# Attention scores as 64x64 products in the quarters of the array, with four scaled tables and a slot of its own for the diagonal

## Chip, cores and metric

The kernel runs on one core of one Trainium2 chip. The metric is the device time of one execution in microseconds (us); less is better. One profiled execution of the kernel before gives the trace that is read here.

## The reference

Three layers follow each other: banded attention, a mixture of experts with soft slots, and a mixture of experts with Sinkhorn weights. All arrays are float32. The parts that the change touches are the scores of the attention and, in the last layer, some small steps that prepare an expert.

```python
# attention: batch 4, 8 heads, 576 positions, head size 64, window 128
scores = q @ k.T / 8
bias = -slopes[h] * |i - j|, slopes[h] = 2.0 ** -(h + 1)
mask = (i - j >= 0) & (i - j < 128)
attn = softmax(where(mask, scores + bias, -1e9))
x = (attn @ v), heads laid side by side -> [2304, 512]

# layer 2: 8 experts with 4 slots each, F = 1024
logits = x @ phi                               # [2304, 32]
slot_input = softmax(logits over rows).T @ x
slot_out[e] = relu(slot_input[e] @ w1[e]) @ w2[e]
x = softmax(logits over slots) @ slot_out

# layer 3: 8 experts, F = 1024
P = exp(x @ w_gate); 8 rounds of: rows to sum 1, columns to sum 1, times N / E
out = sum over e of P[:, e] * (relu(x @ m1[e]) @ m2[e])
```

## The kernel before, in words

The order of all instructions is written out by hand; each engine works through its own queue in that order and waits by semaphores. Loads and stores are issued from SyncE's queue (SP).

**Attention.** The 576 rows of a batch are 9 chunks of 64. Two batches (j = 0, 1) are worked on together, so there are 18 steps t, and a step has two half-steps s = 2t + hf, each for four heads: two groups g = 2 hf + gg of two heads a = 0, 1. `load_nat(t)` (L124) loads a chunk of k and of q, both batches below each other on the 128 partitions, with two loads each; from the third step on, `scale_q` (L178) multiplies q on GpSimd by -(2^(2g-2)), and in the first two steps the copy out of PSUM does it. `emit_tr` (L147) turns them with TensorE transposes, a pair of heads at a time, into kT and qT. kT holds six chunk places; qT is block-diagonal: VectorE writes head a = 0 to partitions 0 to 63 and columns 0 to 63 (L172), ScalarE writes head a = 1 to partitions 64 to 127 and columns 64 to 127 (L173), and the other two blocks stay zero from one memset (L453). So one full 128x128 product (`emit_qk`, L202) gives the scores of both heads of a pair: four products for a half-step, against up to 192 columns of kT. float32 products are two passes each, so a half-step shows eight matmul records.

`emit_sm` (L206) adds one table of distances (rel_sb, 128x192, the same for all heads), scales, and takes the row minimum, by a VectorE instruction for each pair of group and batch (L221). `emit_exp` (L227), `emit_nm` (L234: divide by the sum, L240), `emit_pt` (L242: transposes L251, copies L252) and `emit_pv` (L255, L276) follow, each a half-step or more later, so that half-step s has the scores of s, the division of s - 1, the transposes of s - 2 and the product with v of s - 3. `emit_pv` uses products with 64 output columns, and with 64 or 128 rows. `emit_x` (L287) and `group` (L357) turn the finished chunks and gather the slots of layer 2. Weights of layer 2 are loaded ahead, one part in each half-step.

**Layer 2** ends with `prep_w1(0)`, which prepares expert 0 of layer 3.

**Layer 3** has 72 rounds m = 9 e + n of seven products each (`step`, L1078; each product is 12 matmuls at L1045). Generators run beside the rounds; at each of the seven places of a round one `next` is taken (L1194). They hold the gate and Sinkhorn (L895, L925) and the preparation of the next expert: `prep_w1` (L678) computes 32 matmuls (L682) into the PSUM tile m, takes the row maximum (L686), spreads it over a diagonal (`spread`, L550: tile dg = identity times the maximum, L553), sums the diagonal over partitions with a matmul of ones (`largest`, L557), takes a power of two (L86), scales the result into sh and sl (L701, L702), and copies these by 16 small transfers into stk (L710). `prep_w2a` (L572) then does the same with the maximum of m2 and its own dg. The tile dg has the tag "sl" in the pool mp, so dg and sl share one place.

```python
def spread(am):
    dg = mp.tile([128, 128], F32, tag="sl", name="dg", bufs=1)
    nc.vector.tensor_scalar_mul(dg, idn, am)
    return dg
...
    sl = mp.tile([128, 256], F16, tag="sl", name="sl", bufs=1)
```

Of the kernel before, what the change touches and what calls it, by code (L numbers as in the profile page):

```python
# [24 lines left out]
def tile_kernel(ctx: ExitStack, tc: tile.TileContext, q, k, v, phi, w1, w2, w_gate, m1, m2, rel, out):  # L25
# [69 lines left out]
    with tc.manual_schedule():  # L95
        with ExitStack() as ab:
# [5 lines left out]
            with ExitStack() as at:  # L102
# [13 lines left out]
                phi_sb = late.tile([128, DC, NS], F32, name="phi_sb")  # L116
                rel_sb = sp.tile([128, 192], F32, name="rel_sb", bufs=1)

                qT = one.tile([128, 4, 2, 128], F32, name="qT")

# [3 lines left out]
                def load_nat(t):  # L124
                    bp, c = divmod(t, NCH)
                    for nm, src in (("k", k), ("q", q)):
                        nt_ = nat.tile([128, H, D], F32, tag=nm + "n", name=nm + "n")
                        for j in range(2):
                            nc.sync.dma_start(
                                out=nt_[CH * j:CH * j + CH],  # L130
                                in_=src[2 * bp + j, :, CH * c:CH * c + CH, :].rearrange("h i d -> i h d"),
                            )
                        natt[nm, t] = nt_
                    if t > 1:
                        scale_q(t)

# [9 lines left out]

                def emit_tr(t, nm, gs=range(4), late_=False):  # L147
                    if nm == "q" and t < 2 and len(gs) > 1:
                        for g in gs:
                            emit_tr(t, nm, [g], g % 2 == 1)  # L150
                        return
                    src = natt[nm, t]
                    ps = ps_t.tile([128, 4, 128], F32, tag="pt", name="pt")
                    for i, g in enumerate(gs):
                        nc.tensor.transpose(
                            ps[:, i, :], src[:, 2 * g:2 * g + 2, :].rearrange("p a d -> p (a d)"), idn)
                    pv_ = ps[:, 0:len(gs), :].rearrange("p g (j i) -> p g j i", j=2)
                    if nm == "k":
                        sl_ = t % 4
                        nc.vector.tensor_copy(out=kT[:, :, :, CH * sl_:CH * sl_ + CH], in_=pv_)  # L160
                        if sl_ < 2 and t >= 4:
                            nc.scalar.copy(out=kT[:, :, :, CH * (sl_ + 4):CH * (sl_ + 5)], in_=pv_)
                    else:
                        g0, g1 = gs[0], gs[-1] + 1
                        if t < 2:
                            if not late_:
                                nc.vector.tensor_scalar_mul(qT[0:64, g0, :, 0:64], pv_[0:64, 0], scales[g0])
                            nc.scalar.mul(qT[64:128, g0, :, 64:128], pv_[64:128, 0], scales[g0])
                            if late_:
                                nc.vector.tensor_scalar_mul(qT[0:64, g0, :, 0:64], pv_[0:64, 0], scales[g0])  # L170
                            return
                        nc.vector.tensor_copy(out=qT[0:64, g0:g1, :, 0:64], in_=pv_[0:64])  # L172
                        nc.scalar.copy(out=qT[64:128, g0:g1, :, 64:128], in_=pv_[64:128])  # L173


                scales = [-(2.0 ** (2 * g - 2)) for g in range(4)]

                def scale_q(t):  # L178
                    for g in range(4):
                        x_ = natt["q", t][:, 2 * g:2 * g + 2, :]  # L180
                        nc.gpsimd.tensor_scalar_mul(x_, x_, scales[g])  # L181

# [7 lines left out]
                def emit_qk(s):  # L190
                    t, hf = divmod(s, 2)
                    c = t % NCH
                    nch = min(c, 2) + 1
                    k0 = CH * ((t - nch + 1) % 4)
                    k1 = k0 + CH * nch
                    col = 192 - (k1 - k0)
                    ps = []
                    for gg in range(2):
                        g = 2 * hf + gg
                        ps.append(ps_s.tile([128, 2, 256], F32, tag="s", name="s"))  # L200
                        for j in range(2):
                            nc.tensor.matmul(ps[gg][:, j, col:192], lhsT=qT[:, g, j, :], rhs=kT[:, g, j, k0:k1],  # L202
                                             start=True, stop=True)
                    sc[s] = (ps, col)

                def emit_sm(s):  # L206
# [8 lines left out]
                    for hh in range(4):  # L215
                        gg, j = divmod(hh, 2)
                        w = 192 - col
# [3 lines left out]
                        nc.vector.tensor_tensor_reduce(  # L221
                            out=runs[hh], in0=ps[gg][:, j, col:192],
                            in1=rel_sb[:, col:192], scale=2.0 ** -(4 * hf + 2 * gg + 1), scalar=3e38,
                            op0=ALU.add, op1=ALU.min, accum_out=mx[:, hh:hh + 1])
# [226 lines left out]
                load_nat(0)  # L451
                nc.sync.dma_start(out=rel_sb, in_=rel)
                nc.gpsimd.memset(qT, 0.0)  # L453
                load_nat(1)
# [5 lines left out]
                emit_tr(0, "k")  # L460
                warm(None, ps, idn, 3)
                emit_tr(0, "q", range(0, 2))
                emit_tr(0, "q", range(2, 4))

# [82 lines left out]
            wsum = {}  # L547
            bound = {}

            def spread(am):  # L550

                dg = mp.tile([128, 128], F32, tag="sl", name="dg", bufs=1)
                nc.vector.tensor_scalar_mul(dg, idn, am)  # L553
# [124 lines left out]
            def prep_w1(e, pool=None, tag=None):  # L678
                ps = pool.tile([128, 512], F32, tag=tag, name="m") if pool is not None else pmt
                for dc in range(DC):  # L680
                    for kk in range(4):
                        nc.tensor.matmul(ps[32 * kk:32 * kk + 32, 0:256], lhsT=st[:, dc, :],  # L682
                                         rhs=w1_at("m1", e, dc, 256 * kk, 256),
                                         start=(dc == 0), stop=(dc == DC - 1), tile_position=(0, 32 * kk))
                am = mp.tile([128, 1], F32, tag="am1", name="am1")
                nc.vector.tensor_reduce(out=am, in_=ps[:, 0:256], axis=AX.X, op=ALU.max, apply_absolute_value=True)  # L686
                dg = spread(am)
# [197 lines left out]
            with ExitStack() as ms:  # L885
                ap_ = ms.enter_context(tc.tile_pool(name="acc", bufs=1, reuse_waits="tile"))
                acc = ap_.tile([128, NT, DM], F32, name="acc")

                pmt = pm.tile([128, 512], F32, name="m")
                sp = ms.enter_context(tc.tile_pool(name="sums", bufs=1, reuse_waits="tile"))  # L890
                pz = ms.enter_context(tc.tile_pool(name="pz", bufs=2, reuse_waits="tile", space=PSUM))
# [3 lines left out]
                def gate():  # L895
# [14 lines left out]
                    for g in range(NG):  # L910
                        nc.tensor.matmul(ps[:, 32 * g:32 * g + 32], lhsT=cTf[:, g, :],
                                         rhs=sgb.rearrange("p a b -> p (a b)"), start=True, stop=True)
                    l2 = ps[:, 0:NT * E]
                    mx = mp.tile([128, 1], F32, tag="mx", name="mx")
# [325 lines left out]
```

## Time and profile before

| what | us |
|---|---|
| median of 3 runs | 984.17 |
| lowest, highest | 983.91, 984.69 |
| profiled execution, its own time | 984.86 |
| profiled execution, span from first to last instruction | 983.1 |
| TensorE busy | 950.5 (97%) |
| VectorE busy | 744.9 (76%) |
| ScalarE busy | 624.4 (64%) |
| GpSimd busy | 574.3 (58%) |

The span is counted from the first instruction; all times of rows are from there. Attention's half-steps run from about 8 us to 158 us, layer 2 to 212 us, layer 3 from there to the end. In rows PE is TensorE's matmul, PEld its weight load, DVE VectorE, ACT ScalarE, POOL GpSimd and SP SyncE; SPq is SyncE's queue, which issues the loads. "x8" counts records that follow each other. A matmul's record is as long as its passage through the array, so records overlap: when the next one can start is read from the starts.

### The profile page before, as it was taken

How to read it: one execution, taken by the hardware profiler on the slowest of the kernel's cores; microseconds unless marked ns; L12 is line 12 of the kernel's file. 1: busy time of each engine (PE TensorE's matmuls, PEld its weight loads, DVE VectorE, ACT ScalarE, POOL GpSimd, SP SyncE). 2: the span in 40 equal slices, each digit the busy share in tenths (PEclk: the TensorE clock that was granted, in tenths of full speed). 3: DMA queues.
4: the chain of work that ended last, by engine and by line, in shares of the span. 5: the costliest groups of instructions: out<-in, count | busy, mean ns of one | idle time of the engine just before them, and what ended most of it. 6: DMA issues, size and time to landing. Idle time of an engine off the chain costs nothing.

```text
span 983.1 us, 24146 instructions
## 1 busy us (share of the span) xinstructions
PE 950.5 (97%) x9341; PEld 814.4 (83%) x9341; DVE 744.9 (76%) x1924; ACT 624.4 (64%) x1529; POOL 574.3 (58%) x685
## 2 busy tenths in 40 slices
PE   8999999889799999999999999999999999999997
PEld 7887886447588888888888888888888888888886
DVE  6988896675697687777777777877777777777775
ACT  5877884746467678766666665766476656664542
POOL 2222210204488568947884797499658956995442
PEclk9999999999899999999999999999999999999999
DMA  8999997970200220031005001300220020001222
GB/s 174 257 226 219 254 281 284 368 267 2 96 1 2 94 90 1 2 109 76 1 2 182 2 1 54 131 2 2 89 95 2 1 94 5 2 2 28 60 44 65
DMA packets 94497, 90.07 MB, mean 92 GB/s; under 512 B 63664, under 2 KB 67632, under 8 KB 94384
## 3 DMA queue, kind: packets, MB, share of 16 engines
q1 hardware_dynamic: 94384, 88.54, 30.9%
q8 instruction: 73, 1.20, 0.5%
q14 instruction: 40, 0.33, 0.1%
HBM read 81.97 MB, written 4.72 MB: 88 GB/s over the span
## 4 chain that ended last, share of the span: by engine, by line
PE 67%; DVE 2%; ACT 0%; issue 0%
PE x L1045 34%; PE y L1045 26%; PE z L973 6%; PE m L682 1%; DVE acc L1059 1%; DVE ops L986 0%; DVE sl L702 0%; ACT sh L701 0%; PE m L557 0%; DVE ar L696 0%; DVE w1i L92 0%; DVE w1p L91 0%; DVE w1p L90 0%; DVE acc L1057 0%; PE m L936 0%
## 5 line engine op out<-in xcount | busy, mean ns | idle before, releaser
L1045 PEld LDWEIGHTS <-ops 128*128 128x128 f16 x6048 | 593.4, 98 | 77.2 <-issue 5.5
L1005 POOL TENSOR_TENSOR ops<-s,ops 128x512 f16<-128x512 f32 x287 | 331.9, 1159 | 234.4 <-ACT ops L1002 196.6
L1045 PE MATMUL x<-w2h,ops 128*128 128x256 f16 x2304 | 415.5, 273 | 4.0 <-DVE acc L1059 3.1
L1045 PE MATMUL y<-w2h,ops 128*128 128x256 f16 x1728 | 319.5, 273 | 0.3 <-POOL ops L1005 0.2
L1002 ACT CAST ops<-s 128x512 f16<-128x512 f32 x288 | 177.8, 618 | 218.5 <-DVE s L998 216.0
L1045 PE MATMUL x<-w2l,ops 128*128 128x256 f16 x1152 | 314.8, 274 | 0.0
L1045 PE MATMUL y<-w2l,ops 128*128 128x256 f16 x864 | 235.6, 273 | 0.0
L1059 DVE SCALAR_TENSOR_TENSOR acc<-x,pe,acc 128x256 f32<-128x256 f32 x252 | 121.8, 483 | 71.1 <-PE x L1045 70.0
L983 ACT ACTIVATE ops<-z 128x512 f16<-128x512 f32 x216 | 128.6, 596 | 36.9 <-PE z L973 34.0
L986 DVE SCALAR_TENSOR_TENSOR ops<-z,ops 128x512 f16<-128x512 f32 x216 | 147.0, 681 | 0.0
L1059 DVE SCALAR_TENSOR_TENSOR acc<-y,pe,acc 128x256 f32<-128x256 f32 x189 | 91.4, 484 | 61.4 <-PE y L1045 60.5
L640 POOL TENSOR_TENSOR w2l<-w,w2h 128x256 f16<-128x256 f32 x168 | 112.9, 676 | 0.0
L998 DVE SCALAR_TENSOR_TENSOR s<-z,r 128x512 f32<-128x512 f32 x144 | 98.2, 682 | 10.3 <-ACT r L994 7.1
L998 DVE SCALAR_TENSOR_TENSOR s<-z,s 128x512 f32<-128x512 f32 x144 | 98.1, 681 | 1.4 <-POOL t L640 0.7
L181 POOL TENSOR_SCALAR qn<-qn 128x128 f32<-128x128 f32 x64 | 33.8, 536 | 100.5 <-DMA qn<-in_q_dram 70.7
L973 PE MATMUL z<-ct,stk 128*128 128x256 f16 x576 | 86.8, 274 | 3.2 <-DVE ops L986 2.5
L643 ACT CAST w2h<-w 128x256 f16<-128x256 f32 x168 | 67.0, 402 | 2.3 <-POOL w L640 2.3
L973 PEld LDWEIGHTS <-stk 128*128 128x128 f16 x576 | 55.6, 98 | 13.1 <-DVE ops L986 3.3
L230 ACT ACTIVATE et<-et,mx 128x192 f32<-128x192 f32 (+2 forms) x144 | 61.3, 434 | 1.2 <-DVE mx L221 1.1
L202 PE MATMUL s<-kT,qT 128*128 128x192 f32 (+2 forms) x288 | 50.2, 317 | 0.1
L221 DVE CUSTOM_DVE_ANT_0 et<-s,rel_sb 128x192 f32<-128x192 f32 (+2 forms) x144 | 40.1, 326 | 8.5 <-PE s L202 8.0
L202 PEld LDWEIGHTS s<-kT,qT 128*128 128x128 f32 x288 | 43.7, 191 | 3.4 <-issue 3.4
(196 smaller groups left out, 949.6 us busy)
## 6 DMA issues: line engine op xcount, KB each, us to landing
w<-in_moe_w_dram SPq DMA_DIRECT2D x68, 512.0 KB, 6.4
w<-in_moe_w_dram SPq DMA_DIRECT2D x14, 2048.0 KB, 8.3
kn<-in_k_dram SPq DMA_DIRECT2D x36, 128.0 KB, 5.4
qn<-in_q_dram SPq DMA_DIRECT2D x36, 128.0 KB, 4.9
v<-in_v_dram SPq DMA_DIRECT2D x18, 256.0 KB, 5.1
out_dram<-acc SPq DMA_DIRECT2D x34, 128.0 KB, 2.4
w<-in_moe_w_dram SPq DMA_DIRECT2D x2, 1024.0 KB, 8.4
stk<-sh SPq DMA_DIRECT2D x56, 16.0 KB, 1.8
```

The lines of the kernel that those rows point to most:

```text
L202: nc.tensor.matmul(ps[gg][:, j, col:192], lhsT=qT[:, g, j, :], rhs=kT[:, g, j, k0:k1], start=True, stop=True)
L230: nc.scalar.activation(out=runs[hh], in_=runs[hh], func=AF.Exp, bias=mx[:, hh:hh + 1], scale=-1.0, accum_out=sm[:, hh:hh + 1])
L640: nc.gpsimd.tensor_tensor(out=out_, in0=x_, in1=y_, op=ALU.subtract)
L643: nc.scalar.copy(out=hi[:, i, r], in_=src[:, r])
L973: nc.tensor.matmul(ps[:, i], lhsT=stk[e][:, 128 * ft:128 * ft + 128], rhs=ct.rearrange("p (a n) t -> p a n t", a=2)[:, :, n, :], start=Tru ...
L983: nc.scalar.activation(out=ops_[m][:, k_, 0], in_=zb(m, i, j), func=AF.Relu)
L986: nc.vector.scalar_tensor_tensor(out=ops_[m][:, k_, 1], in0=zb(m, i, j), scalar=0.0, in1=ops_[m][:, k_, 0], op0=ALU.max, op1=ALU.subtract)
L998: nc.vector.scalar_tensor_tensor(out=new_sum(m, nm), in0=zb(m, i, j), scalar=0.0, in1=o, op0=ALU.max, op1=op)
L1002: nc.scalar.copy(out=ops_[m][:, k_, 0], in_=sm_[m, nm])
L1005: eng.tensor_tensor(out=ops_[m][:, k_, 1], in0=sm_[m, nm], in1=ops_[m][:, k_, 0], op=ALU.subtract)
L1045: nc.tensor.matmul(out_, lhsT=a_[:, k_, l_, i, :], rhs=r_[:, k_, i, :], start=(first and j == 0), stop=(j == 11), skip_group_check=True)
L1059: nc.vector.scalar_tensor_tensor(out=o, in0=ps, scalar=pe_[e][:, t:t + 1], in1=o, op0=ALU.mult, op1=ALU.add)
```

## The change

Each head's scores become two products of 64x64 of their own. qT holds 64 columns in place of 128 and no zeros, and is written by one VectorE copy of 128 partitions; ScalarE's copy, GpSimd's scaling and memset and the scaling copies of the first two steps go. The heads of the second batch are loaded swapped within each pair, by two loads with a stride in place of one, so that its head a lies in the other 64 rows of the array. The eight products of a half-step name their quarter by (first row, first column): (0,0) and (64,64) for batch 0, into the PSUM tile ps[0]; (64,0) and (0,64) for batch 1, into ps[1]. The tiles ps are now by batch, with the groups gg in them. The scale moves from q to the table: four tables, made by four ScalarE multiplications at the start; the table's load goes to the fourth place.

In layer 3 the diagonal dg gets a place of its own in the pool "sums", one more `yield` stands between the 32 matmuls of `prep_w1` (experts 1 to 7) and the row maximum, and one between the gate's matmuls (L911) and theirs (L916).

```diff
-                rel_sb = sp.tile([128, 192], F32, name="rel_sb", bufs=1)
+                rel_sb = one.tile([128, 4, 192], F32, name="rel_sb")
-                qT = one.tile([128, 4, 2, 128], F32, name="qT")
+                qT = one.tile([128, 4, 2, 64], F32, name="qT")
...
                         nt_ = nat.tile([128, H, D], F32, tag=nm + "n", name=nm + "n")
-                        for j in range(2):
-                            nc.sync.dma_start(
-                                out=nt_[CH * j:CH * j + CH],
-                                in_=src[2 * bp + j, :, CH * c:CH * c + CH, :].rearrange("h i d -> i h d"),
-                            )
+                        nc.sync.dma_start(out=nt_[0:CH], in_=src[2 * bp, :, CH * c:CH * c + CH, :].rearrange("h i d -> i h d"))
+                        heads = src[2 * bp + 1, :, CH * c:CH * c + CH, :].rearrange("(g a) i d -> i g a d", a=2)
+                        turned_ = nt_[CH:].rearrange("p (g a) d -> p g a d", a=2)
+                        for a in range(2):
+                            nc.sync.dma_start(out=turned_[:, :, 1 - a, :], in_=heads[:, :, a, :])
                         natt[nm, t] = nt_
-                    if t > 1:
-                        scale_q(t)
...
-                        nc.vector.tensor_copy(out=qT[0:64, g0:g1, :, 0:64], in_=pv_[0:64])
-                        nc.scalar.copy(out=qT[64:128, g0:g1, :, 64:128], in_=pv_[64:128])
+                        nc.vector.tensor_copy(out=qT[:, gs[0]:gs[-1] + 1], in_=pv_)
...
-                    ps = []
+                    ps = [ps_s.tile([128, 2, 256], F32, tag="s", name="s") for _ in range(2)]
                     for gg in range(2):
                         g = 2 * hf + gg
-                        ps.append(ps_s.tile([128, 2, 256], F32, tag="s", name="s"))
                         for j in range(2):
-                            nc.tensor.matmul(ps[gg][:, j, col:192], lhsT=qT[:, g, j, :], rhs=kT[:, g, j, k0:k1],
-                                             start=True, stop=True)
+                            for a in range(2):
+                                r0, c0 = CH * (a ^ j), CH * a
+                                nc.tensor.matmul(ps[j][c0:c0 + CH, gg, col:192], lhsT=qT[r0:r0 + CH, g, j, :],
+                                                 rhs=kT[r0:r0 + CH, g, j, k0:k1], start=True, stop=True,
+                                                 tile_position=(r0, c0))
...
-                        gg, j = divmod(hh, 2)
+                        j, gg = divmod(hh, 2)
...
-                            out=runs[hh], in0=ps[gg][:, j, col:192],
-                            in1=rel_sb[:, col:192], scale=2.0 ** -(4 * hf + 2 * gg + 1), scalar=3e38,
+                            out=runs[hh], in0=ps[j][:, gg, col:192],
+                            in1=rel_sb[:, 2 * hf + gg, col:192], scale=-0.125, scalar=3e38,
...
-                nc.sync.dma_start(out=rel_sb, in_=rel)
-                nc.gpsimd.memset(qT, 0.0)
+                nc.sync.dma_start(out=rel_sb[:, 3, :], in_=rel)
...
                 warm(None, ps, idn, 3)
+                for g in range(4):
+                    nc.scalar.mul(rel_sb[:, g, :], rel_sb[:, 3, :], -(2.0 ** (2 - 2 * g)))
...
+            dgp = [mp, "sl"]
...
-                dg = mp.tile([128, 128], F32, tag="sl", name="dg", bufs=1)
+                pool, tag = dgp
+                dg = pool.tile([128, 128], F32, tag=tag, name="dg", bufs=1)
...
                 am = mp.tile([128, 1], F32, tag="am1", name="am1")
+                if e:
+                    yield
                 nc.vector.tensor_reduce(out=am, in_=ps[:, 0:256], axis=AX.X, op=ALU.max, apply_absolute_value=True)
...
+                sp = ms.enter_context(tc.tile_pool(name="sums", bufs=1, reuse_waits="tile"))
+                dgp[:] = [sp, "dg"]
...
                                          rhs=sgb.rearrange("p a b -> p (a b)"), start=True, stop=True)
+                    yield
                     l2 = ps[:, 0:NT * E]
```

## Rows read from the trace of the kernel before

**Rows 1.** Windows: stretch, busy of PE, PEld, DVE, ACT, POOL, clock, DMA share.

```profile
14.00:146.00 132.00, 128.86 (x1616) 109.34 (x1615) 117.20 (x573) 107.87 (x393) 33.96 (x65) 1.00 1.01 243
...
250.30:256.30 6.00, 0.03 (x2) 0.03 (x1) 0.36 (x2) 0.00 (x0) 0.00 (x0) 0.73 0.15 30
253.10:259.80 6.70, 3.39 (x15) 2.33 (x16) 3.69 (x14) 1.38 (x3) 1.16 (x1) 0.50 0.57 183
...
332.00:425.50 93.50, 92.98 (x865) 82.33 (x866) 71.70 (x143) 68.26 (x141) 69.72 (x80) 1.00 0.14 49
```

**Rows 2.** Chain of work that ended last, share of the span by engine.

```profile
PE 67%; DVE 2%; ACT 0%; issue 0%
```

**Rows 3.** TensorE's groups by shape, the first 240 us: busy, mean ns of one.

```profile
L202 PE MATMUL s<-kT,qT 128*128 128x192 f32 x224 | 41.7, 329 | 0.0
```

**Rows 4.** Timeline of TensorE in attention: start, length, count.

```profile
17.79 0.46 PE L276 MATMUL xp<-ptt,v 64*64 64x64 f32 x16
...
68.82 1.47 PE L202 MATMUL s<-kT,qT 128*128 128x192 f32 x8
...
70.12 0.82 PE L251 MATMUL pt<-idn,et 128*128 128x128 f32 x6
...
70.78 0.60 PE L155 MATMUL pt<-idn,kn 128*128 128x128 f32 x4
...
71.31 1.38 PE L276 MATMUL xp<-ptt,v 128*64 128x64 f32 x32
```

**Rows 5.** VectorE's and ScalarE's groups by shape, the first 200 us.

```profile
L172 DVE COPY qT<-pt 64x256 f32<-64x256 f32 x32 | 13.2, 412 | 3.1 <-PE pt L155 2.3
...
L285 DVE COPY xT<-xp 128x256 f32<-128x256 f32 x36 | 13.3, 408 | 2.2 <-PE xp L276 2.2
```

```profile
L230 ACT ACTIVATE et<-et,mx 128x192 f32<-128x192 f32 x112 | 49.6, 453 | 0.0
...
L173 ACT COPY qT<-pt 64x256 f32<-64x256 f32 x32 | 11.8, 367 | 6.4 <-DVE qT L172 5.8
```

**Rows 6.** VectorE's longest wait from 14 to 158 us: total, times, longest.

```profile
DVE et L221 <- PE s L202: 8.0, 8, 1.9
```

**Rows 7.** SyncE's queue's waits, 14 to 146 us, first and last of eleven.

```profile
SPq L144 <- PE pt L155: 10.8, 3, 6.9
...
SPq L144 <- PE s L202: 0.4, 1, 0.4
```

**Rows 8.** DMA queue, 14 to 146 us: packets, MB, share; and a window.

```profile
q1 hardware_dynamic: 57001, 31.76, 99.7%
```

```profile
95.00:103.20 8.20, 8.20 (x94) 6.38 (x93) 7.99 (x38) 7.37 (x28) 1.24 (x3) 1.00 1.18 252
```

**Rows 9.** Start of attention: timeline of SyncE's queue and TensorE, landing of q.

```profile
5.57 1.31 SPq L129 DMA_DIRECT2D qn<-in_q_dram  x2
...
9.82 0.40 PE L155 MATMUL pt<-idn,qn 128*128 128x128 f32 x2
```

```profile
DMA to landing us min/median/max: 3.4/3.5/3.5
```

**Rows 10.** TensorE's waits up to 18 us: total, times, longest.

```profile
PE pt L155 <- ACT qT L168: 0.8, 2, 0.4
...
PE pt L251 <- ACT qT L168: 0.5, 1, 0.5
```

**Rows 11.** Waits of layer 3, 239 to 262 us: total, times, longest.

```profile
DVE dg L553 <- DMA stk<-sl: 7.0, 1, 7.0
...
PE m L557 <- DVE dg L553: 6.0, 1, 6.0
...
PE z L973 <- DVE ops L986: 0.8, 1, 0.8
```

**Rows 12.** TensorE's and VectorE's waits in one later expert, 332 to 425.5 us.

```profile
PE x L1045 <- DVE acc L1059: 0.5, 1, 0.5
```

```profile
DVE am L686 <- PE m L682: 2.6, 1, 2.6
```

More of the change, by code (lines that the diff above doesn't have):

```diff
@@ L145, in load_v, with emit_tr @@
                     vt[bp, c, j] = t
[L147 to L151, printed above, removed]
+                def emit_tr(t, nm, gs=range(4)):
                     src = natt[nm, t]
@@ L163, in emit_tr @@
                     else:
[L164 to L171, printed above, removed]
-                        nc.vector.tensor_copy(out=qT[0:64, g0:g1, :, 0:64], in_=pv_[0:64])
-                        nc.scalar.copy(out=qT[64:128, g0:g1, :, 64:128], in_=pv_[64:128])
[L176 to L181, printed above, removed]
+                        nc.vector.tensor_copy(out=qT[:, gs[0]:gs[-1] + 1], in_=pv_)
                 sc = {}
@@ L887, in tile_kernel @@
                 acc = ap_.tile([128, NT, DM], F32, name="acc")
+                sp = ms.enter_context(tc.tile_pool(name="sums", bufs=1, reuse_waits="tile"))
+                dgp[:] = [sp, "dg"]
                 pmt = pm.tile([128, 512], F32, name="m")
-                sp = ms.enter_context(tc.tile_pool(name="sums", bufs=1, reuse_waits="tile"))
                 pz = ms.enter_context(tc.tile_pool(name="pz", bufs=2, reuse_waits="tile", space=PSUM))
```

## Prediction

> **What bounds the kernel now.** The chain of waits comes first: two thirds of it is TensorE and almost nothing else has a share [rows 2]. The windows by stage then say how dense TensorE is. In attention, from 14 to 146 us, it is busy 128.86 of 132.0 us; in a later expert of layer 3, 92.98 of 93.5; but from 250.3 to 256.3 it does nothing for 6 us [rows 1]. So a part of the change is worth what it takes from TensorE's queue in attention, and what it takes from TensorE's few waits in layer 3. The reader should see a second thing in the attention window: VectorE is busy 117.2 of 132 us and the DMA share is 1.01 [rows 1], so neither is far behind. The lists of waits tell who held whom: VectorE's largest wait in attention is for the scores themselves [rows 6], and SyncE's queue waits for TensorE to give buffers back [rows 7].
>
> The sum is made against the profiled execution: 984.86 us, which is its span of 983.1 and 1.8 around it. That is 0.7 above the median of the runs; the result is brought to the median at the end.
>
> **The scores.** Eight records of 192 columns begin at 68.82 and the next work at 70.12, so a slot is 1.30 / 8 = 0.1625 us [rows 4]. With quarters there are eight products of two passes, 16 records. How many run at once? The trace has products of 64x64 already: in the first chunk of a batch the product with v uses both row halves and both column halves. There 16 records of 64 columns took 0.46 us [rows 4]. A pass of 64 columns is 0.1625 / 3 = 0.054. The last record's own passage is about 0.22 (six transposes in 0.82 less five slots of (70.78 - 70.12) / 6 = 0.11 leave 0.27 for 128 columns, and 64 are 0.05 shorter). One at a time would be 15 x 0.054 + 0.22 = 1.03, two at a time 0.6, four at a time three rounds and a passage, 0.38. The row is nearest to four. So I take four: 4 rounds x 0.1625 = 0.65. What differs: there the two row halves write two tiles (xp[0] and xp[1]), here (0,0) and (64,64) write different partitions of one tile.
>
> Changing from whole array to column halves costs something: four transposes from 70.78 would be through their slots at 71.22, the product with v begins at 71.31 [rows 4], so 0.09. The scores now stand between transposes on both sides, so two changes, 0.18. A half-step of 192 columns goes from 1.30 to 0.83, by 0.47; there are 224 / 8 = 28 of them [rows 3], 13.2 us. The other eight half-steps have 64 or 128 columns; with slots of 0.11 they go from 0.88 to 0.44 + 0.18, by 0.26, 2.1 us together (for 64 columns this is taken over). TensorE loses 15.3 us of work.
>
> On this point the Trainium skill speaks against the change. TensorEngine Tiling (Array Packing), Restrictions and Gotchas, says that different row tiles cannot access the same PSUM bank at the same time. No row of this trace has two row halves in one tile, so the trace neither bears it out nor refutes it. By that rule the scores would cost what the second rival below says.
>
> **What takes the place of TensorE.** VectorE's work stays: the copy of qT grows from 64 to 128 partitions with the same 256 columns, and a 128-partition copy of 256 columns is 408 ns against 412 [rows 5]. With its 117.2 us it would be the tightest engine of the window, since TensorE would have about 114. So the window can shrink by at most 132 - 117.2 = 14.8 us, and by nothing if another resource holds it. The engines take turns (scores, then minimum, then copies that TensorE waits for), and only TensorE is now as dense as 97.6%. With two engines near their limit I take VectorE at 95%: 117.2 / 0.95 = 123.4, a gain of 8.6 us.
>
> ScalarE loses 11.8 us of copies and gets four multiplications of the table, at about 0.45 us like its 128x192 exponentials [rows 5], 1.8 us, at the start, where it has nothing else to do before the first minimum; if that cover were gone they would cost 1.8. GpSimd's multiplications lay behind the landing of q, so q has their time as room. Their end itself is worth nothing, as TensorE hardly waited for them.
>
> SyncE's queue gets 36 loads more, for each two thirds of a microsecond (1.31 for two [rows 9]): 32 x 0.655 = 21 us in the window. It waits there 42 us in eleven rows, of which the first and last are shown [rows 7]. 42 - 21 - 8.6 leaves 12 us: tight but free. The bytes stay, and their packets fill 99.7% of the DMA engines' time in the window; but other stretches reach a share of 1.18 [rows 8], by which the floor is 132 x 0.997 / 1.18 = 111.5 us. Between 111.5 and 131.6 I go by the lower one, as SyncE waited for buffers and not for transfers to be taken.
>
> At the very start the loads are late: q of the second chunk is issued until 6.88, lands 3.5 after its issue, and is used at 9.82 [rows 9], with almost no room. Four loads more stand before its end, 2.6 us. Against that goes the handing over between VectorE, ScalarE and TensorE in the first two steps, for which TensorE waited 0.8 + 0.5 us [rows 10]. So 1.2 us later (bounds 0 and 2.6).
>
> Attention: -8.6 + 1.2 = **-7.4**, bounds 0 and -14.
>
> **The diagonal.** dg and sl share one place, so for expert 1 VectorE's dg waits 7.0 us for the transfers that read sl, and TensorE waits 6.0 us for dg [rows 11]. Behind dg in VectorE's queue stand the sums and splits of the running round, so everything stops. With a place of its own, dg waits only for the matmul of ones that read the dg before it, and that is long done. The next user of those transfers is stk, first read when expert 1 begins, some 50 us later: nothing is late next. Besides, the granted clock is 0.50 from 253.1 to 259.8 [rows 1], that is 1.2 of 2.4 GHz, after TensorE had stood still; the 3.4 us that it worked in there would take 1.7 less at full clock. So 6.0 + 1.7 = 7.7. A wait of 0.8 for VectorE just before [rows 11] belongs to its arrears, which the yields lessen: 0.8 at most, taken whole. Sum **-8.5**, bounds -6 and -9.
>
> **The yields.** In a later expert VectorE waits 2.6 us at the row maximum for the 32 matmuls, and TensorE afterwards 0.5 for VectorE [rows 12]. One place later the matmuls are done when VectorE arrives. 93.5 - 92.98 = 0.52 [rows 1] for each of experts 2 to 7: **-3.1**, bounds 0 and -4. The preparation ends one place of a round later; it has a whole expert's time. The gate's yield I cost at nothing: there TensorE has other reasons to wait.
>
> **Sum.** -7.4 - 8.5 - 3.1 = -19.0: 984.86 - 19.0 = 965.9 for the profiled execution, **965.2** for the median.
>
> **The rivals.**
>
> Transfers hold attention (chance 0.16). For it: share 1.01 and 99.7% [rows 1, 8]. Against it: SyncE's 42 us of waiting [rows 7]. Attention then keeps its length, and layer 3 alone gains 11.6: 972.6.
>
> Two quarters at a time (0.08), because two row halves in one tile take turns. The scores are then 8 x 0.1625 + 0.18, so 0.18 a half-step more than now, 36 x 0.18 = 6.5; with the start's 1.2 and layer 3's 11.6: 980.3. For it is that this pair has no row; against it, that the rows with 64x64 show both halves at work together [rows 4]. This is where the rule of TensorEngine Tiling (Array Packing) would put it.
>
> One at a time (0.04), the other side. 16 x 0.1625 + 0.18 is 1.48 more for each of 28 half-steps and 16 x 0.11 + 0.18 is 1.06 more for eight: 50 us; 984.2 + 50 + 1.2 - 11.6 = 1024. It decides from (11.6 - 1.2) / 36 = 0.29 us a half-step, that is scores above 1.59 us. Only the row of 0.46 [rows 4] stands against it, but clearly.
>
> The stall at the diagonal moves (0.10): VectorE passes dg and stands at its next instruction that needs late work. Then 1 us is left of the 8.5: 972.7. Against it: the sums behind dg were ready long before.
>
> **How the numbers follow.** The forecast has 0.62. Its own range, from the bounds of attention and layer 3, is 957 to 974. For 8 in 10 the upper end goes to 977, over both rivals near 972.6 and towards the second; what lies beyond, the upper rivals and a change better than all bounds, is under 0.2. No change means within 0.2%, 2 us, which is also about what a measurement of this kernel can tell. Faster: 0.62 + 0.16 + 0.10, and a half of the two-at-a-time case, 0.92. Same: 0.03 of that case. Slower: 0.05, the last rival and a rest.
>
> **What would show it.** Score records of 64*64 whose first records start within a few hundredths of a microsecond, half-steps' scores in about 0.83 us; attention's window with VectorE at 95% and TensorE below it; a SyncE queue with far less waiting; no wait of dg for stk, full clock near 250 us; expert periods of 93.0. Wrong would be it if TensorE waited for k or q in attention, if the score records came in pairs, or if another wait of VectorE filled the place at 250 us.

## The result and the profile after

| | before | after |
|---|---|---|
| median of the runs, us | 984.04 (983.87 to 984.69) | 973.84 (971.82 to 977.32) |
| ratio | | 0.9899, 95% interval 0.9869 to 0.9928 |
| profiled execution / its span, us | 984.86 / 983.1 | 977.32 / 975.5 |
| first product of layer 2 starts at, us | 166.2 | 167.4 |
| first preparation to second preparation in layer 3, us | 92.1 | 87.7 |
| each of the later experts, us | 93.49 | 92.81 |

The change gains 10.2 us where 19.0 were forecast. 973.84 lies inside the range, but the split is another one: in the profiled execution attention, which was to give 7.4, ends 1.2 later, and all that was gained was gained in layer 3. That execution is the slowest of the four, 3.5 above their median, so it may show the late loads at their worst; which part gains what is settled by the first two experiments.

The windows of the changed kernel, for [rows 1] (busy of PE, PEld, DVE, ACT, POOL, clock, DMA share, GB/s):

```profile
14.00:146.00 132.00, 123.31 (x1870) 88.92 (x1862) 113.74 (x566) 95.08 (x361) 0.00 (x0) 0.93 1.04 236
250.30:256.30 6.00, 6.00 (x44) 4.88 (x43) 5.32 (x13) 2.43 (x5) 1.16 (x1) 0.76 0.11 27
326.70:419.50 92.80, 92.80 (x869) 82.32 (x869) 71.44 (x143) 67.91 (x141) 70.04 (x81) 1.00 0.14 50
```

In attention TensorE and VectorE are both less busy than before, GpSimd does nothing any more, the granted clock has fallen from 1.00 to 0.93, and the DMA share is 1.04: none of the compute engines is the bound there. The stall from 250.3 to 256.3 is gone, and the later expert has no wait left on TensorE; but the clock of 0.76 near 250 us is not the full one that was forecast. The chain that ended last, for [rows 2], is still TensorE's:

```profile
PE 69%; DVE 0%; issue 0%
```

TensorE's timeline in the steady part of attention, for [rows 4] (start, length), and the scores' group of [rows 3]:

```profile
69.53 0.88 PE L183 MATMUL s<-kT,qT 64*64 64x192 f32 x16
70.34 0.87 PE L233 MATMUL pt<-idn,et 128*128 128x128 f32 x6
71.05 0.60 PE L151 MATMUL pt<-idn,kn 128*128 128x128 f32 x4
71.58 1.38 PE L258 MATMUL xp<-ptt,v 128*64 128x64 f32 x32
72.89 0.44 PE L151 MATMUL pt<-idn,qn 128*128 128x128 f32 x2
73.26 0.39 PE L183 MATMUL s<-kT,qT 64*64 64x192 f32 x4
```

```profile
L183 PE MATMUL s<-kT,qT 64*64 64x192 f32 x448 | 25.8, 348 | 0.0
```

The 16 records of the scores take 0.88 us, and what follows starts 0.81 after their begin: four quarters run at once. The records start in rounds of four, 7 ns apart within a round; the rounds begin 0, 0.21, 0.38 and 0.54 us after the first record. (0,0) and (64,64) write one tile of 2 KB a partition at the same time here, so the rule of the Trainium skill's TensorEngine Tiling (Array Packing), Restrictions and Gotchas, that was weighed in the prediction, does not show as time in this trace. The half-step is 73.26 - 69.53 = 3.73, before 72.90 - 68.82 = 4.08.

Where the pace is kept, then, 0.35 us a half-step are gained. It is not kept everywhere. TensorE's timeline at the start of the changed kernel, and its largest waits of the first 165 us (total, times, longest):

```profile
8.15 0.46 PE L183 MATMUL s<-kT,qT 64*64 64x64 f32 x16 [0.30 <-DVE qT L160]
9.84 0.63 PE L151 MATMUL pt<-idn,kn 128*128 128x128 f32 x4 [1.22 <-DMA kn<-in_k_dram]
11.50 0.66 PE L151 MATMUL pt<-idn,qn 128*128 128x128 f32 x2 [1.04 <-DMA qn<-in_q_dram]
12.09 0.71 PE L183 MATMUL s<-kT,qT 64*64 64x64 f32 x16
```

```profile
PE pt L151 <- ACT et L212: 2.3, 1, 2.3
PE pt L151 <- DVE et L222: 2.2, 2, 1.7
...
PE pt L151 <- DMA qn<-in_q_dram: 1.3, 2, 1.0
```

TensorE waits for k and for q of position 1, which the prediction named as what would make it wrong. After those waits the granted clock is 0.50, that is 1.2 of 2.4 GHz, from 10.9 to 24.5 us, and twice more for 3.4 us in attention (from 103.0 and 130.3), in half-steps that take 6.6 and 8.5 us. The timeline has a long wait in both of these:

```profile
102.81 0.90 PE L151 MATMUL pt<-idn,kn 128*128 128x128 f32 x4 [2.25 <-ACT et L212]
...
129.62 0.63 PE L151 MATMUL pt<-idn,kn 128*128 128x128 f32 x4 [1.74 <-DVE et L222]
```

The releasers named work on et, which a transpose of k doesn't read. What came just before is the load: k of position 13 lands at 102.7, that of position 16 at 129.4, so the load is taken to be what ended both waits. From position 2 on, k lies ready 0.1 to 2.2 us before its use; in the kernel before it was 1.6 to 9.1.

SyncE's queue and the DMA queue, from 14 to 146 us, for [rows 7, 8] (wait: total, times, longest; transfers: count, KB each, median us from issue to landing):

```profile
SPq L130 <- PE pt L233: 6.3, 9, 1.5
```

```profile
q1 hardware_dynamic: 58398, 30.90, 102.7%
...
kn<-in_k_dram SPq DMA_DIRECT2D x15, 128.0 KB, 6.5
kn<-in_k_dram SPq DMA_DIRECT2D x30, 64.0 KB, 5.7
```

The queue's waits add up to 20.6 us, where the prediction left 12 of 42. But its issues have grown too: before, 113 loads took it 100.0 of the 132 us; now 148 take 118.3. Most take 0.6 to 0.66 us; 36 of the 148 take longer than 0.8 (28 of the 113 before). Waits and issues overlap in this account: before, 42 and 100.0 us are more than the 132 us of the window.

VectorE's waits in attention, for [rows 6], and the copies of [rows 5]:

```profile
DVE et L203 <- PE s L183: 10.2, 12, 1.6
DVE qT L160 <- PE pt L151: 6.6, 7, 1.9
DVE kT L156 <- PE pt L151: 6.0, 4, 3.9
```

```profile
L160 DVE COPY qT<-pt 128x256 f32<-128x256 f32 x36 | 15.0, 419 | 6.7 <-PE pt L151 6.6
```

It now waits longer for transposes of q (2.3 us before) and for those of k, which wait for loads. The waits of layer 3 from 239 to 262 us, for [rows 11]:

```profile
PE z L962 <- DVE ops L975: 2.2, 1, 2.2
DVE am L673 <- PE m L925: 1.8, 1, 1.8
```

dg no longer waits for stk. But VectorE still waits 1.8 us at the row maximum of expert 1, now for another product (L925, the column sums of the normalisation, which go into the same tile pmt), and TensorE's wait for VectorE's ops grew from 0.8 to 2.2. It ends at 249.3, and from 249.8 to 253.2 the granted clock is 0.50.

### The profile page after: what moved, and what is told of

It is laid out like the page before. It is cut to its first block, busy times and chain, and to the rows that moved or that the text cites. A ratio compares the mean times of both kernels' runs of the same rounds, so it can differ in the third digit from the quotient of the medians.

```text
span 975.5 us, 24588 instructions
## 1 busy us (share of the span) xinstructions
PE 940.9 (96%) x9629; PEld 790.9 (81%) x9629; DVE 741.7 (76%) x1920; ACT 611.8 (63%) x1493; POOL 540.2 (55%) x620
## 4 chain that ended last, share of the span: by engine, by line
PE 69%; DVE 0%; issue 0%
PE x L1034 35%; PE y L1034 27%; PE z L962 6%; PE m L667 1%; PE m L542 0%; DVE ops L975 0%; DVE acc L1048 0%; DVE acc L1046 0%; PE m L925 0%
## 5 line engine op out<-in xcount | busy, mean ns | idle before, releaser
L972 ACT ACTIVATE ops<-z 128x512 f16<-128x512 f32 x216 | 128.6, 596 | 35.7 <-PE z L962 33.2
L203 DVE CUSTOM_DVE_ANT_0 et<-s,rel_sb 128x192 f32<-128x192 f32 (+2 forms) x144 | 39.5, 331 | 10.3 <-PE s L183 10.2
L258 PE MATMUL xp<-ptt,v 64*64 64x64 f32 (+1 forms) x1024 | 45.5, 244 | 1.5 <-DVE cn L328 0.5
L234 ACT COPY ptt<-pt 128x384 f32<-128x384 f32 (+2 forms) x72 | 28.6, 445 | 28.7 <-PE pt L233 28.6
```

Of the source, the lines that this page charges most:

```text
L258: nc.tensor.matmul(xp[j][64 * a:64 * a + 64, g, :], lhsT=vt[bp, vc, j][r0:r1, 2 * g + a, :], rhs=ptt[r0:r1, gg, 128 * blk + 64 * a:128 * b ...
L972: nc.scalar.activation(out=ops_[m][:, k_, 0], in_=zb(m, i, j), func=AF.Relu)
```

## The experiments

Theory at the start: the added loads take from attention what the scores give. Rivals: the scores or VectorE give less than was worked out; or the change of layer 3 takes something back.

**The two parts apart.** The first kernel is the one before with the part of layer 3 (slot and yields); the second is the changed one without it.

> The kernel before with the layer-3 part of the change alone (the diagonal's own place and the two yields). The prediction's terms: 8.5 + 3.1, 972.5. If the trace of the changed kernel is right, in which layer 3 from the first product to the end is 9.0 shorter than before: 975.0. The rival, that the stall only moves: 980 or more.

> The changed kernel without the layer-3 part. If attention gained nothing from the change, as the starts of layer 2 say (167.4 against 166.2): 984 to 986. By the prediction's term for attention: 976.6.

| | median, us | ratio to before (984.27) |
|---|---|---|
| layer 3 alone | 975.23 | 0.9910 (0.9898 to 0.9923) |
| attention alone | 984.88 | 1.0010 (0.9997 to 1.0024) |

The first is at the 975.0 that the trace of the changed kernel gave, not at the prediction's 972.5 and not at the rival's 980. The whole gain is layer 3's. Attention alone gains nothing and scatters (981.8 to 990.2). Its profile, of a run of 983.68, has the half clock at the start (11.4 to 25.1 us) and the two long half-steps of the changed kernel as well, of 5.8 and 6.2 us; layer 2 starts at 165.5.

**One load for the second batch.** Two DMAs become one, with the same bytes.

```diff
-                        for a in range(2):
-                            nc.sync.dma_start(out=turned_[:, :, 1 - a, :], in_=heads[:, :, a, :])
+                        nc.sync.dma_start(out=nt_[CH:], in_=src[2 * bp + 1, :, CH * c:CH * c + CH, :].rearrange("h i d -> i h d"))
```

> The changed kernel with one load for the second batch in place of two, its heads not swapped, so that the second batch's scores are those of the neighbouring head (bytes and all other work are as in the changed kernel). Theory: the 72 loads more in SyncE's queue make k and q late, and TensorE waits for them; without them attention ends 7 to 10 us sooner, 964 to 967, and the slack between a chunk's landing and its use is 2 us or more. Rival, the DMA engines' throughput holds attention: the bytes are the same, so 972 to 975. Rival, VectorE and TensorE hold each other: 972 to 975 as well, with slack in the loads.

968.34 us, ratio 0.9837 (0.9824 to 0.9849): 5.5 less than the changed kernel; layer 2 starts at 159.7 instead of 167.4. The number lies a little above the range of the load theory and clearly below that of the rivals: the 36 added loads (not 72; that is the number of all loads of the second batch in the changed kernel) cost most of the 8.6 that are missing from the forecast, not all of it. The slack of 2 us or more that the theory named did not come: from position 2 on, k lies ready only 0.1 to 2.4 us before its use here as well. Without the added loads the queue is late by less; the lead is not back.

**The added loads from GpSimd's queue.**

```diff
-                            nc.sync.dma_start(out=turned_[:, :, 1 - a, :], in_=heads[:, :, a, :])
+                            nc.gpsimd.dma_start(out=turned_[:, :, 1 - a, :], in_=heads[:, :, a, :])
```

> The changed kernel with the second batch's two loads issued from GpSimd's queue, which has nothing to do in attention. If it is the time that SyncE's queue takes to issue: 964 to 968, as with one load. If it is the number or size of the transfers themselves: 972 to 976.

1087.7 us, ratio 1.1045: a miss for every theory. GpSimd's timeline and its waits say why:

```profile
23.15 0.63 POOL L134 DMA_DIRECT2D qn<-in_q_dram  x1 [1.96 <-issue]
25.73 0.61 POOL L134 DMA_DIRECT2D kn<-in_k_dram  x1 [1.96 <-issue]
28.28 0.63 POOL L134 DMA_DIRECT2D kn<-in_k_dram  x1 [1.93 <-issue]
```

```profile
POOL qn L134 <- issue: 53.9, 17, 5.8
```

The 72 loads start 2.5 us apart at the least and 3.5 on average, waits for buffers included, so a position's four take GpSimd 10 us or more where TensorE wants a position every 7.5. The run says nothing on SyncE.

**No added loads, and the right result.** Both batches are loaded whole; the second batch's heads come out exchanged in the scores' second tile. A second table and the other column half in the product with v put that right, and q is scaled in the copy of qT, half on VectorE, half on ScalarE.

```diff
-                                r0, c0 = CH * (a ^ j), CH * a
+                                r0, c0 = CH * a, CH * (a ^ j)
...
-                        nc.vector.tensor_copy(out=qT[:, gs[0]:gs[-1] + 1], in_=pv_)
+                        s0, s1 = (-(2.0 ** (2 * g - 2)) for g in gs)
+                        nc.vector.tensor_scalar_mul(qT[:, gs[0]], pv_[:, 0], s0)
+                        nc.scalar.mul(qT[:, gs[1]], pv_[:, 1], s1)
...
-                                    rhs=ptt[r0:r1, gg, 128 * blk + 64 * a:128 * blk + 64 * a + 64],
+                                    rhs=ptt[r0:r1, gg, 128 * blk + 64 * (a ^ j):128 * blk + 64 * (a ^ j) + 64],
```

> The changed kernel without its four-part loads: k and q of the second batch are loaded whole, as before, and their heads come out exchanged in the scores' second tile instead; a second table with its halves exchanged and the other column half in the product with v put that right. q is scaled in the copy of qT, one pair of heads on VectorE, one on ScalarE. Theory 'the added loads ate the gain': 965 to 969 us, the time of the run in which the second batch was loaded by one DMA, because no load is added. Rival 'the copies of qT': two engines write one qT, and TensorE waited for ScalarE's qT in the kernel before; then some 0.1 us per half-step comes back, 36 of them, 969 to 972. Rival 'the gain was never in the loads but in the data order of that run': 973 to 975.

968.25 us, ratio 0.9837 (0.9824 to 0.9851), as the load theory had it: the gain does not hang on the wrong heads of the run before. In its profile layer 2 starts at 157.2, 9.0 earlier than in the kernel before.

**Where the added loads hurt.** The changed kernel, with one unturned load for the second batch in the first two positions, or in all but these.

```diff
+                        if t < 2:
+                            nc.sync.dma_start(out=nt_[CH:], in_=src[2 * bp + 1, :, CH * c:CH * c + CH, :].rearrange("h i d -> i h d"))
+                            natt[nm, t] = nt_
+                            continue
```

> The changed kernel, with the second batch's heads loaded by one DMA each, not exchanged, in the first two of the 18 positions alone (these positions' scores of the second batch go to the wrong heads); the other 16 as in the change. Theory 'the start': the added loads hurt where SyncE's queue issues one load after the other and TensorE waits for each, and where its clock then falls to half (10.9 to 24.5 us in the changed kernel); most of the difference of 5.5 us comes back, 968 to 970. Rival 'throughout': each of the 18 positions loses its 0.3 us; two of them give back 0.6, 973 to 974.

> The complement: the first two positions loaded as in the change, the other 16 with one DMA for the second batch, not exchanged (their scores of the second batch go to the wrong heads). Theory 'the start': little is gained, 971.5 to 974, and the half clock after 10.9 us stays. Rival 'throughout': 968 to 970, and no stretch of half clock is needed to explain the rest.

971.24 us (0.9850 to 0.9879) and 972.29 us (0.9856 to 0.9891). Neither theory: the first lies between both ranges; the second lies in that of 'the start', but its half clock is not the one from 10.9 us (12.6 to 16.1 and 29.7 to 36.5 in its profile). Each gives back a part, and the two can't be told apart. What the first two positions won was lost again a little later. TensorE's timeline of the first of the two kernels:

```profile
24.73 1.16 PE L237 MATMUL pt<-idn,et 128*128 128x128 f32 x6
28.68 1.09 PE L155 MATMUL pt<-idn,kn 128*128 128x128 f32 x4 [2.80 <-DMA kn<-in_k_dram]
```

It meets the next late load, k of position 4, waits 2.8 us, and the clock is 0.50 from 28.1 to 34.9.

**The clock by itself.** Idle products keep TensorE at work during the two waits for position 1.

```diff
+                        if s == 0:
+                            warm(ps_t, "pt", idn, 6)
                         if t + 1 < NT and hf == 0:
                             emit_tr(t + 1, "k")
+                        if s == 0:
+                            warm(ps_t, "pt", idn, 5)
```

> The changed kernel with eleven idle products of 128 columns put into TensorE's two waits for the loads of position 1 (1.22 and 1.04 us), so that it works on while it waits. Loads are as in the change. Theory 'half of the start's price is the clock': no half clock from 10.9 to 24.5, and 1.5 to 3 us come back, 971 to 972.5. Rival 'the loads alone set it': the clock stays full, the waits for loads grow by as much, 973.5 to 975.

975.7 us (974.83 to 978.7): nothing comes back, as the rival had it, a little above its range. TensorE's timeline of this kernel:

```profile
14.54 0.49 PE L233 MATMUL pt<-idn,et 128*128 128x128 f32 x2 [0.45 <-DVE et L222]
16.44 1.09 PE L151 MATMUL pt<-idn,kn 128*128 128x128 f32 x4 [1.42 <-DMA kn<-in_k_dram]
```

The clock holds until 16.1 us and then is 0.50 for 10.2 us, behind the next wait for k; the rival's full clock did not come. The half clock follows the waits for late loads, and lifting it for a while brings nothing as long as they are late. What the idle products themselves cost was not measured.

**The same number of loads, fewer bytes.** The weights that are fetched ahead are cut to a quarter.

```diff
+            if thin:
+                nc.gpsimd.memset(wt[nm, e], 0.0)
...
+        f = src.shape[2] // (4 if thin else 1)
-        nc.sync.dma_start(out=t.rearrange("p (c f) -> p c f", c=n)[:, n0:n1, :], in_=src[:, n0:n1, :])
+        nc.sync.dma_start(out=t.rearrange("p (c f) -> p c f", c=n)[:, n0:n1, 0:f], in_=src[:, n0:n1, 0:f])
```

> The changed kernel with the weights fetched ahead during attention cut to a quarter of their columns (the other columns are zero, set by GpSimd, which has nothing else to do there); the number of transfers and their order on SyncE's queue stay. Each part falls from 512 to 128 KB, so a half-step of attention moves about 0.53 MB instead of 0.91. Theory 'bytes': the loads of k and q land 5 to 6 us after their issue because the weights' bytes are ahead of them; attention gets 4 to 7 us shorter, 967 to 970. Rival 'issue': SyncE takes 0.64 us for each load whatever its size, so with the same count nothing is gained, 973 to 975.

987.59 us, and both were missed, for a reason that has nothing to do with the question. VectorE's copies of sel (duration in ns: least, median, longest) and GpSimd's timeline:

```profile
L443 DVE COPY sel<-idn x4: 170/175/27860, 1.3 to 29.6; 32x32 f32<-32x32 f32 x4
```

```profile
1.39 27.69 POOL L61 MEMSET w<- 128x4096 f32 x8
```

One copy of 32x32 that takes 0.17 us otherwise took 27.9, until GpSimd's memsets were done; TensorE's scores waited 23.5 us for VectorE. Behind that, the run does answer. From its first scores (30.9) to the start of its last (159.8) attention takes 128.9 us; the changed kernel takes 140.1, the one before 138.5. Its loads from 14 to 146 us:

```profile
kn<-in_k_dram SPq DMA_DIRECT2D x15, 128.0 KB, 3.7
kn<-in_k_dram SPq DMA_DIRECT2D x30, 64.0 KB, 3.2
```

They land in 3.2 to 3.7 us instead of 5.7 to 6.5, k lies ready 3 to 11 us ahead from position 3 on, and an issue takes SyncE 0.67 us on average instead of 0.80. So with every added load in place attention keeps its pace when the weights' bytes are not in the way. Two reservations: by the freeze, the loads of positions 1 and 2 had 20 us of lead; and the weights' own issues became shorter with their size (1.03 us on average, now 0.64), so the run doesn't part bytes from issue time.

**The weights later.** The kernel without added loads, with the fetching ahead begun at the seventh half-step instead of the third.

```diff
-                        if s > 2 and pre:
+                        if s > 6 and pre:
```

> The kernel without added loads (two tables, heads exchanged in the scores' second tile), with the weights' fetching begun four half-steps later, at the seventh instead of the third; all weights are fetched as before. In its profile two half-steps from 23.2 us take 5.8 and 4.7 us where 2.8 to 3.7 is the pace. Theory 'the weights crowd the loads of k and q while attention starts': 3 us less, 964.5 to 966.5. Rival 'the pace of the buffers': the same, 967.5 to 969.5. Against both: the last weights come later than layer 2 wants them, 970 and more.

965.08 us, ratio 0.9823 (0.9798 to 0.9847): the lowest median of the study, in the range of the first theory. Against 968.25 the intervals overlap (its runs reach from 964.5 to 972.7), so the 3 us are not shown by the times; its profile shows the mechanism: the half-steps of 5.8 and 4.7 us are now 3.7 and 4.0, the clock is full from 5 us to the end of attention, and from the first to the last scores it takes 127.9 us. Layer 2 begins at 154.0 instead of 157.2; from there to the first product of layer 3 it takes 47.4 us, 1.6 more, and the rest stays. Attention's window in this kernel:

```profile
14.00:146.00 132.00, 128.27 (x2094) 94.29 (x2094) 115.61 (x596) 108.47 (x415) 0.00 (x0) 1.00 1.04 252
```

Beside this run the profile of the changed kernel tells where late loads cost. Its attention is 12.2 us longer (140.1 against 127.9): 5.9 of them in the first seven half-steps, up to 33.2 us, and 6.2 in the two half-steps at 98.7 and 125.7, in which the late k of positions 13 and 16 is waited for. Between, from 33.2 to 98.7, it keeps the pace (65.5 us against 64.9).

**Slot and yields apart**, each in the kernel before.

> The kernel before with one part of the change: the diagonal's own slot in layer 3, and neither of the two yields. The prediction's term for it was 8.5 us: 975.5 to 976.5. The traces of the kernels with the whole layer-3 part show 4.8 to 5.3 us less up to the preparation of expert 2, and 4.1 to 4.25 less after it. Rival 'the slot is worth what lies ahead of expert 2 alone': 979 to 980.

> The kernel before with the two yields of layer 3 alone; the diagonal keeps the slot that it shares. The prediction's term for it was 3.1 us, 0.52 in each of six experts: 980.5 to 981.5. If the later experts gain 0.68 each, as they do with the whole part, 980 to 980.5. Rival 'the yield without the slot gives the diagonal's transfer more time ahead of it, and so takes part of the 6 us too': 976 to 979. Rival 'the row maximum comes later and with it the wait for the shared slot': 984 and more.

| | median, us | ratio to before (984.58) | first to second preparation | a later expert |
|---|---|---|---|---|
| slot alone | 977.57 | 0.9929 (0.9916 to 0.9942) | 85.0 | 93.49 |
| yields alone | 982.20 | 0.9976 (0.9967 to 0.9985) | 94.1 | 92.81 |
| both | 975.23 | 0.9910 (0.9898 to 0.9923) | 86.4 | 92.81 |

Waits from 236 to 262 us, with the slot alone and with the yields alone:

```profile
PE z L976 <- DVE ops L989: 0.8, 1, 0.8
```

```profile
DVE dg L553 <- DMA stk<-sl: 7.2, 1, 7.2
...
PE m L557 <- DVE c L942: 6.5, 1, 6.5
...
PE z L976 <- DVE ops L989: 2.2, 1, 2.2
```

Both times lie between the ranges that were named: the slot gives less than the prediction's term and more than the rival's, the yields less than their term, and the rivals of the yields did not come. The slot takes the 6 us stall away. The yields win 0.68 in each of six later experts, 4.1, and cost in expert 1: 1.4 with the slot, 2.0 without it. The two yields were not tried one without the other; that of the gate is taken once only, so the later experts' gain is that of `prep_w1`'s.

## Why the prediction was half right

*The scores.* Right: four quarters at once, 0.81 us to what follows, 0.83 predicted. Mis-sized: the half-step lost 0.35, not 0.47. The 0.81 are four rounds of 0.1625, 0.05 more in the first and 0.11 more from the last round to the next work. The two changes of mode stood inside the 0.83, but the row shows cost on top of it: the transposes behind the scores take 0.71 instead of 0.66 to what follows, the last transposes before them 0.37 instead of 0.28. Where loads don't disturb, attention gains 138.5 - 127.9 = 10.6 us, where TensorE's work was to shrink by 15.3.

*VectorE as the next bound, taken at 95%.* Wrong, though its 8.6 is not far from 10.6. In the kernel with the later weights TensorE is busy 128.27 of 132 us and VectorE 115.61, 88%; but there ScalarE makes half of the copies of qT. With all of them on VectorE the run with thin weights is the one to read:

```profile
31.00:157.00 126.00, 120.42 (x1902) 87.68 (x1902) 115.33 (x587) 96.98 (x371) 0.00 (x0) 0.98 0.66 153
```

TensorE is busy 96% there, VectorE 92%: TensorE is still the denser one.

*SyncE's queue "tight but free".* This is the step that failed. The sum counted the queue's waiting (42 us) as room into which 32 loads of 0.655 fit. Even taken as room it was too much: the records of the issues before fill 100.0 of the 132 us, so at most 32 lie between them, and 32 - 21 - 8.6 leaves 2.4, not 12. And the queue issues in order, and an issue is not a landing: with the DMA engines at a share above 1, k and q land 4.9 to 6.5 us after their issue (5.5 and 5.6 before), and every added load is issued 0.65 us behind another. What had been waiting in the queue was the lead of the loads over TensorE, for k 1.6 to 9.1 us, and a faster TensorE and 35 more issues used it up. That the DMA floor was put aside was right: the kernel without added loads moves 33.89 MB through the queue in the same window, the one before 31.76. Fewer loads (5.5 us back), fewer bytes beside them (half-steps at pace) and, in the kernel without added loads, later bytes (the two slow half-steps at the start gone, 3 us in the medians, which the noise could hide) each relieve it. The lead itself came back only with the later weights: for k 3.4 to 7.8 us in positions 5 to 12. How one added load's price divides between issue and transfer is still open: the run with thin weights had its head start, and the one on another queue says nothing on it.

*The start, +1.2.* Right sign, too small. The scores of position 1 start 2.0 us later (12.09, before 10.06), and behind that come the half clock and the next late loads.

*The diagonal, -8.5.* Measured -7.0 by itself. The stall and its half clock went; the wait of 0.8 for VectorE's ops, taken whole, is still there, and with the yields it grows to 2.2.

*The yields, -3.1.* Measured -2.4 by themselves (interval 1.5 to 3.2). The later experts gave more than was worked out, 0.68 against 0.52 each; left out was that expert 1's row maximum then waits behind the column sums of the normalisation, 1.4 to 2.0 us. A yield for the experts from 2 on alone should give these 1.4 us; it was not tried.

*The rivals.* "Transfers hold attention" gave 972.6, close to 973.84, with a chance of 0.16, and attention did keep its length. What held it was not the share of the DMA engines that it argued from, though: with the same bytes in fewer loads 5.5 us came back. The argument against it, SyncE's 42 us of waiting, was the mistake. Two at a time and one at a time did not come, and the stall at the diagonal did not move: the slot by itself gives 7.0.

*The range.* That 973.84 lies in it is luck as far as attention goes: the forecast of 965.2 counted on 7.4 from attention, which gave nothing, and the range reached far enough up because it was drawn over rivals.

## What to carry to other kernels

Waiting time in an in-order load queue is not free room if it is the lead of loads over their use: before adding loads, take from the trace how long each tile lies ready before it is used, and what that lead is once the consumer is faster. A layout that could be put right at the consumer (another quarter, another table, another column half) was better here than one put right by more loads, 968.25 against 973.84. A bulk prefetch that shares the queue is worth trying later, after the start-up, when the short loads have their lead; here it gave 965.08 against 968.25, with overlapping intervals.

## What the runs showed of the hardware

GpSimd's memsets stopped a VectorE copy for as long as they lasted: 27.9 us for a 32x32 copy, across eight memsets of 3.5 us in a row. The Trainium skill's SBUF — State Buffer, Who interferes with whom, says that a copy can run in a mode in which VectorE contends with GpSimd for a shared port pair, and that the loser blocks for the whole instruction; this trace agrees in that the copy stands blocked, and shows that with memsets back to back it waits for all of them; which mode the copy ran in, the trace does not show.

Loads issued by GpSimd started 2.5 us apart at the least; most issues of SyncE took 0.6 to 0.66 us. Some of SyncE's take longer for the same kind of load (64 KB of k: 0.6 to 2.1 us in the changed kernel). The mean over all its loads was 0.80 us with the whole weights and 0.67 with a quarter, most of the difference in the issues of the weights themselves; what makes an issue long is not shown.
